# A hand-ordered list of steps that begins at unit 22 instead of unit 19

## The chip, the cores and the metric

The kernel runs on one core of one Trainium2 chip. The metric is the device time of one execution in microseconds.

## The reference

Attention with a position bias for 8 batches and 8 heads of 576 positions with 64 values each, followed by a soft mixture of 8 experts. Everything is float32.

```python
scores = scale * np.matmul(q, k.transpose(0, 1, 3, 2))
x = (psi_rel / psi_i)[..., None]
bias = np.maximum(x @ w1 + b1, 0.0) @ w2
scores = scores + bias.transpose(2, 0, 1)[None, :, :, :]
attn = np.exp(scores - np.max(scores, axis=-1, keepdims=True))
attn = attn / (np.sum(attn, axis=-1, keepdims=True) + 1e-09)
x = np.matmul(attn, v)                       # then laid out as (4608, 512)
logits = x @ phi
d = softmax of logits over the rows          # dispatch
slot_input = d.T @ x                         # 8 experts of 4 slots
slot_out = np.maximum(slot_input[e] @ w1[e], 0.0) @ w2[e]
c = softmax of logits over the slots         # combine
return c @ slot_out
```

## The kernel before

The heads go in four pairs, and a **unit** is one pair of heads of one batch: 32 units, units 0 to 7 for the first pair, 8 to 15, 16 to 23 and 24 to 31 for the last. Ahead of them stand the position biases, which go to DRAM and are read back for each pair; behind them the experts' two layers and the output.

A unit is cut into short named steps, each of one engine (or of SyncE's queue, for transfers):

- `lq`, `lv`: load of q and k (two buffers), of v (two buffers); `wf`: fetch of a block of expert weights, 512 KB, in units 8 to 23; `b0` to `b4`: the bias tiles of the next pair, in its last unit
- for each of five row blocks p: `S` scores (TensorE), `t` bias add and row minimum (VectorE, one for each head), `e` exponential with row sums (ScalarE), `m` reciprocal (VectorE), `n` scaling (GpSimd), `T` and `R` transposes (TensorE), `c`, `cr`, `cR` copies out of PSUM (ScalarE, or VectorE where the mark says so)
- for the two halves: `M0.0` to `M0.4` and `M1.0` to `M1.4`, the products with v (TensorE), `x0`, `x1` copies of the result, and `xs`, the store to the DRAM tensor `xs` for the first three pairs
- for the units of the last pair: `fx`, the read-back of the other pairs' results of that batch, `K`, `L`, `D` and so on for the experts' dispatch
- `w21` to `w36`, filed under unit 31: fetches of weights into buffers of other tiles as these come free

Which block of weights a fetch brings follows from the count of the fetches before it.

All steps are sorted by a place, and the program is issued in that order with no rescheduling, so that each engine's queue is the sorted list of its own steps. The place comes from one of two sources: the list `END`, if the step stands in it (place 1000 and up, in the list's order), or the formula `5 * u + PLAIN[n]`, which lets every unit repeat one pattern, with the end of a unit's work (the M1 steps, whose `PLAIN` is 8.997 to 10.445) among the next unit's first steps.

```python
place, eng = max(rank[u, n] if (u, n) in rank else (5 * u + PLAIN[n][0], PLAIN[n][1]) for n in names.split())
prog.append((place, len(prog), lambda: f(eng)))
...
for _, _, f in sorted(prog, key=lambda x: x[:2]):
    f()
```

In the kernel before, the list names all steps of units 19 to 31, but for the weight fetches of units 22 and 23. Whatever the list does not name stands in front of it. So the last steps of unit 18, `M1.0` to `M1.4`, `x1` and `xs`, all stand in front of the first step of unit 19, and so do the fetches `wf/22` and `wf/23`: the order at that place is

```
... T3/18 cR3/18 c3/18 M1.0/18 M1.1/18 M1.2/18 M1.3/18 M1.4/18 x1/18+ xs/18 wf/22 wf/23
| w21/31 lq/20 lv/19 wf/19 S0/19 S1/19 t0.0/19 t0.1/19 e0.0/19 t1.0/19 S2/19 e0.1/19 fx/24 ...
```

with the list behind the bar. Profile lines: `S` is L379 (L375 for block 4), `t` L392, `e` L399, `m` L407 and L408, `n` L321, `T` and `R` L357, copies L324, `M` L482, `xs` L494, `fx` L505, `lq` L298, `lv` L303, bias tiles L311 to L317, weight fetches L778.

Of the kernel before, what the change touches and what calls it, by code (L numbers as in the profile page):

```python
# [40 lines left out]
}  # L41

END = """
w21/31 lq/20 lv/19 wf/19 S0/19 S1/19 t0.0/19 t0.1/19 e0.0/19 t1.0/19 S2/19 e0.1/19 fx/24 e1.0/19 m0/19 t1.1/19 n0.1/19
e1.1/19 n0.0/19 m1/19 T0/19 t2.0/19 S4/19 n1.0/19 c0/19 t2.1/19 n1.1/19 e2.1/19 R1/19 S3/19 cR1/19+ e2.0/19 t4.0/19
lq/21 t3.0/19 e4.0/19 S0/20 lv/20 t3.1/19 wf/20 T1/19 m4/19 e3.1/19 m2/19 t0.0/20 e3.0/19 n2.1/19 t0.1/20 c1/19
n2.0/19 m3/19 n4.0/19 T2/19 e0.0/20 n4.1/19 S1/20 c2/19 n3.1/19 T4/19 n3.0/19 e0.1/20 t1.0/20 M0.0/19 M0.1/19 c4/19
m0/20 M0.2/19 t1.1/20 e1.0/20 n0.1/20 M0.3/19 M0.4/19 cr4.0/19 n0.0/20 e1.1/20 cr4.1/19+ R3/19 T3/19 x0/19+ cR3/19
S2/20 m1/20 c3/19 n1.0/20 T0/20 n1.1/20 t2.0/20 S4/20 c0/20 t2.1/20 R1/20 e2.1/20 S3/20 cR1/20+ t4.0/20 e2.0/20
M1.0/19 lq/22 t3.0/20 e4.0/20 M1.1/19 t3.1/20 M1.2/19 m4/20 e3.1/20 S0/21 m2/20 e3.0/20 n2.1/20 T1/20 n2.0/20 M1.3/19  # L50
c1/20 t0.0/21 M1.4/19 n4.0/20 t0.1/21 n4.1/20 e0.0/21 T2/20 lv/21 x1/19+ S1/21 wf/21 m3/20 c2/20 xs/19 n3.1/20 T4/20
e0.1/21 n3.0/20 M0.0/20 t1.0/21 M0.1/20 c4/20 m0/21 M0.2/20 e1.0/21 t1.1/21 M0.3/20 n0.1/21 M0.4/20 cr4.0/20 e1.1/21
n0.0/21 cr4.1/20+ R3/20 T3/20 x0/20+ cR3/20 S2/21 m1/21 c3/20 n1.0/21 T0/21 n1.1/21 t2.0/21 S4/21 c0/21 t2.1/21 R1/21
e2.1/21 S3/21 cR1/21+ t4.0/21 e2.0/21 M1.0/20 lq/23 t3.0/21 e4.0/21 M1.1/20 t3.1/21 M1.2/20 m4/21 e3.1/21 S0/22 m2/21
e3.0/21 n2.1/21 T1/21 n2.0/21 M1.3/20 c1/21 t0.0/22 M1.4/20 n4.0/21 t0.1/22 n4.1/21 e0.0/22 T2/21 lv/22 x1/20+ S1/22
m3/21 xs/20 c2/21 n3.1/21 T4/21 e0.1/22 n3.0/21 M0.0/21 t1.0/22 M0.1/21 c4/21 m0/22 M0.2/21 e1.0/22 t1.1/22 M0.3/21
n0.1/22 M0.4/21 cr4.0/21 e1.1/22 n0.0/22 cr4.1/21+ R3/21 T3/21 x0/21+ cR3/21 S2/22 m1/22 c3/21 n1.0/22 T0/22 n1.1/22
t2.0/22 S4/22 c0/22 t2.1/22 R1/22 e2.1/22 S3/22 cR1/22+ t4.0/22 e2.0/22 M1.0/21 t3.0/22 e4.0/22 M1.1/21 t3.1/22
M1.2/21 m4/22 e3.1/22 S0/23 m2/22 e3.0/22 n2.1/22 T1/22 n2.0/22 M1.3/21 c1/22 t0.0/23 M1.4/21 n4.0/22 t0.1/23 n4.1/22
e0.0/23 lq/24 T2/22 lv/23 x1/21+ S1/23 m3/22 c2/22 xs/21 n3.1/22 T4/22 e0.1/23 b2/23 n3.0/22 M0.0/22 t1.0/23 M0.1/22  # L60
c4/22 m0/23 M0.2/22 e1.0/23 t1.1/23 M0.3/22 n0.1/23 M0.4/22 cr4.0/22 e1.1/23 n0.0/23 cr4.1/22+ R3/22 T3/22 x0/22+
cR3/22 S2/23 m1/23 c3/22 n1.0/23 T0/23 n1.1/23 t2.0/23 S4/23 c0/23 t2.1/23 b1/23 R1/23 e2.1/23 S3/23 cR1/23+ t4.0/23
b3/23 e2.0/23 M1.0/22 t3.0/23 e4.0/23 M1.1/22 t3.1/23 M1.2/22 m4/23 e3.1/23 m2/23 lq/25 b0/23 e3.0/23 n2.1/23 T1/23
S2/24 t2.0/24 n2.0/23 M1.3/22 c1/23 M1.4/22 n4.0/23 n4.1/23 t2.1/24 T2/23 S1/24 x1/22+ e2.0/24 T4/23 m3/23 c2/23
e2.1/24 n3.1/23 n3.0/23 M0.0/23 t1.0/24 M0.1/23 c4/23 b4/23 M0.2/23 M0.3/23 t1.1/24 M0.4/23 e1.0/24 cr4.0/23 cr4.1/23+
R3/23 T3/23 x0/23+ e1.1/24 S0/24 cR3/23 m2/24 m1/24 c3/23 t0.0/24 t0.1/24 n2.0/24 n2.1/24 n1.0/24 S3/24 e0.0/24
t3.0/24 M1.0/23 M1.1/23 lv/24 M1.2/23 M1.3/23 M1.4/23 T2/24 e0.1/24 n1.1/24 t3.1/24 m0/24 x1/23+ T1/24 e3.1/24 e3.0/24
m3/24 c2/24 n0.1/24 n0.0/24 T0/24 c0/24 S4/24 R1/24 c1/24+ S0/25 t4.0/24 n3.0/24 n3.1/24 R3/24 cR1/24 cR3/24 T3/24
t0.0/25 c3/24 S2/25 t0.1/25 t2.0/25 e4.0/24 S1/25 M0.0/24 m4/24 M0.1/24 n4.0/24 n4.1/24 M0.2/24 t1.0/25 M0.3/24
t1.1/25 e0.0/25 T4/24 e2.0/25 e0.1/25 e1.1/25 t2.1/25 c4/24+ e2.1/25 cr4.0/24 S3/25 M0.4/24 cr4.1/24 m0/25 e1.0/25  # L70
M1.0/24 t3.0/25 e3.0/25 m1/25 m2/25 t3.1/25 M1.1/24 xs/22 lq/26 lv/25 e3.1/25 x0/24+ M1.2/24 n0.1/25 n0.0/25 n1.1/25
M1.3/24 M1.4/24 n1.0/25 m3/25 x1/24+ T0/25 n2.0/25 R1/25 n2.1/25 c0/25 T1/25 cR1/25+ K01/24 c1/25 S2/26 kc01/24+
t2.0/26 n3.1/25 n3.0/25 t2.1/26 T2/25 S4/25 c2/25 t4.0/25 R3/25 S1/26 cR3/25 e2.1/26 e4.0/25 t1.0/26 S0/26 T3/25
t1.1/26 L/24 m4/25 t0.0/26 M0.0/25 e2.0/26 n4.0/25 M0.1/25 c3/25 n4.1/25 T4/25 t0.1/26 lc/24+ e0.0/26 S3/26 e1.1/26
e0.1/26 m2/26 c4/25+ M0.2/25 cr4.0/25 cr4.1/25+ e1.0/26 D/24 m0/26 t3.0/26 d1/24 m1/26 M0.3/25 M1.0/25 M0.4/25 t3.1/26
n0.1/26 M1.1/25 lv/26 xs/23 M1.2/25 n2.1/26 n2.0/26 n0.0/26 n1.1/26 n1.0/26 e3.0/26 d2/24 M1.3/25 e3.1/26 x0/25+
M1.4/25 dq/24 KR/24 T0/26 K23/24 x1/25+ d3/24 R1/26 krc/24 S4/26 c0/26+ cR1/26 kc23/24 m3/26 t4.0/26 T1/26 lq/27 S2/27
c1/26 T2/26 M0.0/26 M0.1/26 t2.0/27 M0.2/26 lv/27 M0.3/26 W/24 lq/28 c2/26 fx/25 t2.1/27 n3.1/26 M0.4/26 n3.0/26
x0/26+ e4.0/26 m4/26 e2.1/27 T3/26 wc/24 e2.0/27 n4.0/26 R3/26 cR3/26 S0/27 t0.0/27 c3/26 t0.1/27 Z/24 S1/27 zc/24
n4.1/26 e0.0/27 e0.1/27 t1.0/27 K01/25 kc01/25 L/25 t1.1/27 T4/26 lc/25 S3/27 m0/27 c4/26+ K23/25 cr4.0/26+ cr4.1/26+  # L80
t3.0/27 e1.1/27 e1.0/27 D/25 M1.0/26 t3.1/27 kc23/25 M1.1/26 m1/27 m2/27 d1/25 C/24 e3.1/27 e3.0/27 M1.2/26 cA/24
M1.3/26 d2/25 M1.4/26 m3/27 n0.1/27 n0.0/27 n1.0/27 n1.1/27 n2.1/27 n2.0/27 cB/24 dq/25 KR/25 x1/26+ T0/27 n3.1/27
n3.0/27 krc/25+ c0/27 W/25 R1/27 wc/25+ T2/27 S2/28 cR1/27 c2/27 T1/27 fx/26 S4/27 d3/25 t2.0/28 t2.1/28 c1/27 R3/27
cR3/27+ S0/28 t4.0/27 e4.0/27 T3/27 Z/25 t0.0/28 t0.1/28 m4/27 K01/26 c3/27 n4.0/27 S1/28 e0.0/28 zc/25 kc01/26
t1.0/28 L/26 K23/26 e0.1/28 t1.1/28 lc/26 n4.1/27 m0/28 T4/27 kc23/26 c4/27+ cr4.0/27+ cr4.1/27 S3/28 e1.1/28 e1.0/28
e2.0/28 e2.1/28 M0.0/27 D/26 t3.0/28 t3.1/28 C/25 cC/24 m1/28 M0.1/27 n1.1/28 d1/26 M1.0/27 M1.1/27 M0.2/27 e3.1/28
n0.0/28 n0.1/28 M0.3/27 M0.4/27 d2/26 M1.2/27 M1.3/27 n1.0/28 cA/25 M1.4/27 m2/28 e3.0/28 x0/27 d3/26 dq/26+ W/26
# [903 lines left out]
```

## Time and profile before

| | us |
|---|---|
| median of 3 runs | 636.65 |
| lowest and highest | 636.62, 640.1 |
| the profiled execution | 636.0 |
| its span, first to last instruction | 634.2 |

A row gives times in us (mean lengths of one instruction in ns); PE is TensorE, PEld its weight loads, DVE VectorE, ACT ScalarE, POOL GpSimd, SPq SyncE's queue, which issues the DMAs. "Granted clock" is TensorE's clock as a share of full speed. An instruction's row in order of time merges like neighbours (x8: eight of them), and its length then runs from the first to the last.

### The profile page before, as it was taken

What the parts mean: (1) busy time and instruction counts of PE and PEld (TensorE: products, weight loads), DVE (VectorE), ACT (ScalarE), POOL (GpSimd) and SP (SyncE); (2) the same over time, 40 slices, a digit from 0 to 9 for tenths busy, and PEclk for the clock granted to TensorE, in tenths of its full rate; (3) what the DMA queues carried; (4) which work ended last, traced back from release to release, by engine and by line L of the source; (5) the groups of instructions that cost most, each with busy time, mean ns of one, the idle gap of its engine ahead of it and who ended that gap; (6) DMA issues with size and microseconds to landing.
All of it is one profiled execution on the core that took longest, in us unless ns stands there. A gap on an engine that the chain in (4) does not pass through costs nothing.

```text
span 634.2 us, 18241 instructions
## 1 busy us (share of the span) xinstructions
PE 599.0 (94%) x7079; PEld 374.6 (59%) x7079; DVE 427.2 (67%) x1331; ACT 481.8 (76%) x987; POOL 224.7 (35%) x336
## 2 busy tenths in 40 slices
PE   6999699999999999999987999999999999999883
PEld 3444466666666666666654666666666666543452
DVE  7997767767666666666636667677778887664043
ACT  6998788888888888888847888877877778532142
POOL 0000554455555445555424544644314343100000
PEclk9999899999999999999998999999999999999897
DMA  6777222233855453594318326432233137879998
GB/s 237 244 243 251 75 81 82 85 114 117 247 193 169 146 171 128 160 289 133 113 44 337 115 80 179 149 101 64 94 118 118 54 122 244 278 243 352 347 364 299
DMA packets 54694, 110.71 MB, mean 175 GB/s; under 512 B 7120, under 2 KB 24784, under 8 KB 54608
## 3 DMA queue, kind: packets, MB, share of 16 engines
q1 hardware_dynamic: 54608, 109.54, 52.5%
q8 instruction: 56, 0.92, 0.6%
q14 instruction: 30, 0.25, 0.1%
HBM read 82.39 MB, written 27.13 MB: 173 GB/s over the span
## 4 chain that ended last, share of the span: by engine, by line
PE 87%; DVE 4%; ACT 4%; issue 2%; DMA 1%; POOL 1%; SPq 0%; ACTq 0%; POOLq 0%; DVEq 0%
PE ps L482 25%; PE ps L379 20%; PE ps L357 16%; PE ps L274 8%; PE ps L375 6%; PE ps L894 3%; PE ps L869 2%; ACT y L399 2%; PE ps L548 1%; DVE y L392 1%; PE ps L924 1%; PE ps L678 1%; ACT at L324 1%; PE ps L846 1%; DMA tabs<-in_tab_dram 1%
## 5 line engine op out<-in xcount | busy, mean ns | idle before, releaser
L321 POOL TENSOR_SCALAR y<-y,sm 128x576 f32<-128x576 f32 (+1 forms) x320 | 221.9, 707 | 318.6 <-DVE sm L408 194.7
L399 ACT ACTIVATE y<-y,mn 128x576 f32<-128x576 f32 x288 | 222.1, 772 | 37.2 <-DVE sm L407 19.3
L392 DVE CUSTOM_DVE_ANT_0 y<-ps,bm 128x576 f32<-128x576 f32 x256 | 185.2, 754 | 95.5 <-PE ps L357 52.8
L324 ACT COPY at<-ps 128x1024 f32<-128x1024 f32 (+3 forms) x211 | 153.7, 733 | 39.4 <-PE ps L357 31.2
L482 PE MATMUL ps<-at,v 128*64 128x320 f32 (+1 forms) x1280 | 175.3, 413 | 1.3 <-ACT at L324 1.1
L379 PE MATMUL ps<-qk 64*128 64x288 f32 x1024 | 157.3, 423 | 0.0
L357 PEld LDWEIGHTS ps<-ident,y 64*128 64x128 f32 x2624 | 104.4, 139 | 62.5 <-POOL y L321 22.2
L357 PE MATMUL ps<-ident,y 64*128 64x64 f32 x2624 | 119.0, 227 | 10.3 <-POOL y L321 7.8
L482 PEld LDWEIGHTS ps<-at,v 128*64 128x64 f32 x1280 | 83.8, 136 | 61.4 <-issue 9.6
L379 PEld LDWEIGHTS ps<-qk 64*128 64x128 f32 x1024 | 94.4, 189 | 25.6 <-DVE sm L407 9.8
L274 PE MATMUL ps<-f,wbd 128*32 128x512 f32 (+1 forms) x576 | 52.6, 419 | 2.4 <-DVE f L257 2.4
L399 ACT ACTIVATION_READ_ACCUMULATOR y<-y,mn 128x1 f32 x288 | 54.1, 188 | 0.0
L257 DVE TENSOR_SCALAR f<-tabs,scl,nb 128x576 f32<-128x576 f32 x106 | 52.1, 587 | 0.5 <-DMA tabs<-in_tab_dram 0.5
L324 DVE COPY at<-ps 128x256 f32<-128x256 f32 (+3 forms) x77 | 33.7, 442 | 21.7 <-PE ps L357 15.5
L274 PEld LDWEIGHTS ps<-f,wbd 128*32 128x32 f32 x576 | 25.6, 110 | 29.4 <-issue 17.0
L375 PE MATMUL ps<-qk 64*64 64x288 f32 x256 | 39.9, 432 | 0.0
L324 DVE COPY xts<-ps 128x256 f32<-128x256 f32 (+1 forms) x57 | 25.9, 454 | 15.7 <-PE ps L482 12.9
L254 ACT ACTIVATE f<-tabs,cols,scl 128x576 f32<-128x576 f32 x38 | 33.3, 888 | 0.0
L407 DVE TENSOR_SCALAR sm<-sm 128x2 f32<-128x2 f32 (+1 forms) x160 | 28.1, 176 | 3.9 <-ACT y L399 3.3
L408 DVE RECIPROCAL sm<-sm 128x2 f32<-128x2 f32 (+1 forms) x160 | 26.4, 165 | 5.5
L278 ACT ACTIVATE e<-ps,bcon 128x576 f32<-128x576 f32 x36 | 27.2, 757 | 1.6 <-PE ps L274 0.6
L392 DVE CUSTOM_DVE_ANT_0 y<-ps,br 128x576 f32<-128x576 f32 x32 | 24.0, 749 | 1.5 <-PE ps L357 1.0
(147 smaller groups left out, 368.1 us busy)
## 6 DMA issues: line engine op xcount, KB each, us to landing
wt<-in_moe_w_dram SPq DMA_DIRECT2D x64, 512.0 KB, 6.2
qk<-in_qk_dram SPq DMA_DIRECT2D x32, 608.0 KB, 3.8
v<-in_v_dram SPq DMA_DIRECT2D x32, 320.0 KB, 3.3
bias_m<-e SPq DMA_DIRECT2D x32, 288.0 KB, 2.9
out_dram<-ob SPq DMA_DIRECT2D x16, 512.0 KB, 5.2
xs<-xts SPq DMA_DIRECT2D x24, 288.0 KB, 4.8
xo<-xs SPq DMA_DIRECT2D x8, 864.0 KB, 5.7
bm<-bias_m SPq DMA_DIRECT2D x16, 288.0 KB, 4.1
```

The costliest lines, as they stand in the source:

```text
L254: nc.scalar.activation(out=f, in_=tabs[:, s0:s0 + S], func=AF.Relu, bias=cols[:, 1:2], scale=scl[:, sc:sc + 1])
L257: nc.vector.tensor_scalar(out=f, in0=tabs[:, s0:s0 + S], scalar1=scl[:, sc:sc + 1], scalar2=nb1[:, 0:1], op0=ALU.mult, op1=ALU.max)
L274: nc.tensor.matmul(pb[32 * t:32 * t + 32, n, 0:w], wbd, fb[t][:, 512 * n:512 * n + w], start=True, stop=True, tile_position=(0, 32 * t))
L321: nc.gpsimd.tensor_scalar(out=out, in0=y, scalar1=r, scalar2=1.0, op0=ALU.mult, op1=ALU.mult)
L324: (nc.vector.tensor_copy if eng else nc.scalar.copy)(out=out, in_=in_)
L357: nc.tensor.matmul(out, src[rs], ident[rs, rs], is_transpose=True, start=True, stop=True, tile_position=(64 * r, 0))
L375: nc.tensor.matmul(pss[0].t[rs, n, 0:HALF], x[rs, 1152:1216], x[rs, 64 + n * HALF:64 + (n + 1) * HALF], start=True, stop=True, tile_positi ...
L379: nc.tensor.matmul(pss[hh].t[:, n, 0:HALF], x[rs, 640 + p * P:640 + (p + 1) * P], x[rs, k0:k0 + HALF], start=True, stop=True, tile_positio ...
L392: nc.vector.tensor_tensor_reduce(out=d["y", p][:, hs].rearrange("a (x n) -> a x n", x=2), in0=t[:, :, 0:HALF], in1=biases[hp][p][:, hs].re ...
L399: nc.scalar.activation(out=y, in_=y, func=AF.Exp, bias=d["mn", p][:, hh:hh + 1], scale=-1.0, accum_out=d["sm", p][:, hh:hh + 1])
L407: nc.vector.tensor_scalar(out=r, in0=r, scalar1=1e-9, scalar2=None, op0=ALU.add)
L482: nc.tensor.matmul(po[64 * hh:64 * hh + 64], d["v"][:, v0:v0 + 64], main[:, :, 4 * hh + i, :] if i < 4 else rest, start=i == 0, stop=i == ...
```

## The change

Only the text of `END` is changed. The steps of units 19 to 21, the first part of unit 22 and a few of unit 23 are taken out of the list, so that the formula places them; the list now begins at the load of q and k for unit 24, which is issued while unit 23 begins. In front of that load stand `w21/31`, which began the list before, and `fx/24`, the first read-back. `wf/23` is put behind the load of v for unit 23; `wf/22` falls to its place by the formula. All other entries keep their order.

```diff
 END = """
-w21/31 lq/20 lv/19 wf/19 S0/19 S1/19 t0.0/19 t0.1/19 e0.0/19 t1.0/19 S2/19 e0.1/19 fx/24 e1.0/19 m0/19 t1.1/19 n0.1/19
...
-e3.0/22 n2.1/22 T1/22 n2.0/22 M1.3/21 c1/22 t0.0/23 M1.4/21 n4.0/22 t0.1/23 n4.1/22
-e0.0/23 lq/24 T2/22 lv/23 x1/21+ S1/23 m3/22 c2/22 xs/21 n3.1/22 T4/22 e0.1/23 b2/23 n3.0/22 M0.0/22 t1.0/23 M0.1/22
...
+w21/31 fx/24 lq/24 T2/22 lv/23 wf/23 x1/21+ S1/23 m3/22 c2/22 xs/21 n3.1/22 T4/22 e0.1/23 b2/23 n3.0/22 M0.0/22
+t1.0/23 M0.1/22 c4/22 m0/23 M0.2/22 e1.0/23 t1.1/23 M0.3/22 n0.1/23 M0.4/22 cr4.0/22 e1.1/23 n0.0/23 cr4.1/22+ R3/22
...
```

With the formula's places written out, the order around the list's new first entry is

```
... lv/22 wf/22 c1/21 x1/20+ xs/20 S1/22 ... e3.0/22 M1.1/21 M1.2/21 S0/23 m2/22 T1/22 M1.3/21 n2.1/22 n2.0/22
t0.0/23 t0.1/23 n4.0/22 M1.4/21 n4.1/22 c1/22 e0.0/23
| w21/31 fx/24 lq/24 T2/22 lv/23 wf/23 x1/21+ S1/23 m3/22 c2/22 xs/21 n3.1/22 T4/22 e0.1/23 b2/23 ...
```

## Rows read from the trace of the kernel before

**Rows 1.** The page: busy time by engine, and the chain's share by engine

```profile
PE 599.0 (94%) x7079; PEld 374.6 (59%) x7079; DVE 427.2 (67%) x1331; ACT 481.8 (76%) x987; POOL 224.7 (35%) x336
...
PE 87%; DVE 4%; ACT 4%; issue 2%; DMA 1%; POOL 1%; SPq 0%; ACTq 0%; POOLq 0%; DVEq 0%
```

**Rows 2.** SyncE's queue in order of time: start, length (us), line, what is issued

```profile
294.74 0.33 SPq L303 DMA_DIRECT2D v<-in_v_dram  x1
...
308.47 0.33 SPq L303 DMA_DIRECT2D v<-in_v_dram  x1
...
372.05 0.33 SPq L303 DMA_DIRECT2D v<-in_v_dram  x1
...
385.74 0.33 SPq L303 DMA_DIRECT2D v<-in_v_dram  x1
```

**Rows 3.** By stretch: length, each engine's busy time (instructions), TensorE's granted clock, DMA share, GB/s

```profile
102.54:308.47 205.93, 205.93 (x2432) 136.26 (x2434) 138.33 (x481) 180.41 (x376) 104.06 (x151) 1.00 0.50 157
...
294.74:308.47 13.73, 13.73 (x164) 9.09 (x166) 9.20 (x33) 12.02 (x26) 6.93 (x11) 1.00 0.43 130
...
308.47:385.74 77.27, 71.51 (x812) 46.10 (x814) 46.22 (x161) 59.87 (x126) 34.63 (x51) 0.98 0.42 141
...
358.37:372.05 13.68, 13.68 (x164) 9.02 (x166) 9.19 (x33) 12.01 (x26) 6.94 (x11) 1.00 0.44 131
```

**Rows 4.** TensorE in order of time, in brackets the idle time before and its releaser

```profile
327.19 2.91 PE L482 MATMUL ps<-at,v 128*64 128x320 f32 x20 [1.11 <-ACT at L324]
...
335.96 0.82 PE L357 MATMUL ps<-ident,y 64*128 64x64 f32 x16 [1.82 <-POOL y L321]
...
344.48 0.71 PE L357 MATMUL ps<-ident,y 64*128 64x64 f32 x16 [2.15 <-DVE sm L407]
```

**Rows 5.** GpSimd in order of time, the same columns

```profile
334.44 1.47 POOL L321 TENSOR_SCALAR y<-y,sm 128x576 f32<-128x576 f32 x2 [10.57 <-DVE sm L408]
```

**Rows 6.** By stretch, the old join, columns as in rows 3

```profile
331.04:344.73 13.69, 9.72 (x86) 5.94 (x86) 9.65 (x33) 9.03 (x20) 4.71 (x7) 0.88 0.96 353
...
336.00:340.00 4.00, 4.00 (x33) 2.33 (x34) 2.17 (x8) 2.53 (x5) 1.47 (x2) 0.57 1.04 417
```

**Rows 7.** SyncE's queue in order of time, columns as in rows 2

```profile
334.30 0.58 SPq L505 DMA_DIRECT2D xo<-xs  x1
...
372.81 0.33 SPq L494 DMA_DIRECT2D xs<-xts  x1
...
381.11 0.33 SPq L298 DMA_DIRECT2D qk<-in_qk_dram  x1
...
387.86 0.46 SPq L313 DMA_DIRECT2D bm<-bias_m  x1
```

**Rows 8.** DMA issues: line, count, KB each, median us from issue to landing

```profile
wt<-in_moe_w_dram SPq DMA_DIRECT2D x64, 512.0 KB, 6.2
...
qk<-in_qk_dram SPq DMA_DIRECT2D x32, 608.0 KB, 3.8
...
xo<-xs SPq DMA_DIRECT2D x8, 864.0 KB, 5.7
...
bm<-bias_m SPq DMA_DIRECT2D x16, 256.0 KB, 4.5
```

**Rows 9.** TensorE and VectorE in order of time, the first readers behind the new join

```profile
396.98 1.19 PE L379 MATMUL ps<-qk 64*128 64x288 f32 x8
...
398.30 0.76 DVE L392 CUSTOM_DVE_ANT_0 y<-ps,bm 128x576 f32<-128x576 f32 x1 [1.45 <-PE ps L379]
```

**Rows 10.** By stretch, columns as in rows 3

```profile
372.05:385.74 13.69, 13.69 (x164) 9.02 (x166) 9.20 (x33) 12.01 (x26) 6.94 (x11) 1.00 0.30 93
...
385.74:399.44 13.70, 13.70 (x165) 8.87 (x166) 9.23 (x33) 12.03 (x26) 6.94 (x11) 1.00 0.77 227
...
580.00:590.00 10.00, 7.03 (x58) 3.50 (x54) 1.84 (x3) 4.43 (x6) 0.00 (x0) 0.95 1.10 348
...
590.00:600.00 10.00, 9.44 (x140) 4.81 (x134) 0.42 (x1) 0.61 (x2) 0.00 (x0) 0.88 1.11 348
```

More of the change, by code (lines that the diff above doesn't have):

```diff
@@ L43 @@
 END = """
-w21/31 lq/20 lv/19 wf/19 S0/19 S1/19 t0.0/19 t0.1/19 e0.0/19 t1.0/19 S2/19 e0.1/19 fx/24 e1.0/19 m0/19 t1.1/19 n0.1/19
[L45 to L58, printed above, removed]
@@ L59 @@
-M1.2/21 m4/22 e3.1/22 S0/23 m2/22 e3.0/22 n2.1/22 T1/22 n2.0/22 M1.3/21 c1/22 t0.0/23 M1.4/21 n4.0/22 t0.1/23 n4.1/22
-e0.0/23 lq/24 T2/22 lv/23 x1/21+ S1/23 m3/22 c2/22 xs/21 n3.1/22 T4/22 e0.1/23 b2/23 n3.0/22 M0.0/22 t1.0/23 M0.1/22
-c4/22 m0/23 M0.2/22 e1.0/23 t1.1/23 M0.3/22 n0.1/23 M0.4/22 cr4.0/22 e1.1/23 n0.0/23 cr4.1/22+ R3/22 T3/22 x0/22+
-cR3/22 S2/23 m1/23 c3/22 n1.0/23 T0/23 n1.1/23 t2.0/23 S4/23 c0/23 t2.1/23 b1/23 R1/23 e2.1/23 S3/23 cR1/23+ t4.0/23
-b3/23 e2.0/23 M1.0/22 t3.0/23 e4.0/23 M1.1/22 t3.1/23 M1.2/22 m4/23 e3.1/23 m2/23 lq/25 b0/23 e3.0/23 n2.1/23 T1/23
@@ L64 @@
[L64 to L83, printed above, removed]
@@ L84 @@
-cR3/27+ S0/28 t4.0/27 e4.0/27 T3/27 Z/25 t0.0/28 t0.1/28 m4/27 K01/26 c3/27 n4.0/27 S1/28 e0.0/28 zc/25 kc01/26
+w21/31 fx/24 lq/24 T2/22 lv/23 wf/23 x1/21+ S1/23 m3/22 c2/22 xs/21 n3.1/22 T4/22 e0.1/23 b2/23 n3.0/22 M0.0/22
+t1.0/23 M0.1/22 c4/22 m0/23 M0.2/22 e1.0/23 t1.1/23 M0.3/22 n0.1/23 M0.4/22 cr4.0/22 e1.1/23 n0.0/23 cr4.1/22+ R3/22
+T3/22 x0/22+ cR3/22 S2/23 m1/23 c3/22 n1.0/23 T0/23 n1.1/23 t2.0/23 S4/23 c0/23 t2.1/23 b1/23 R1/23 e2.1/23 S3/23
+cR1/23+ t4.0/23 b3/23 e2.0/23 M1.0/22 t3.0/23 e4.0/23 M1.1/22 t3.1/23 M1.2/22 m4/23 e3.1/23 m2/23 lq/25 b0/23 e3.0/23
@@ new lines @@
+n2.1/23 T1/23 S2/24 t2.0/24 n2.0/23 M1.3/22 c1/23 M1.4/22 n4.0/23 n4.1/23 t2.1/24 T2/23 S1/24 x1/22+ e2.0/24 T4/23
+m3/23 c2/23 e2.1/24 n3.1/23 n3.0/23 M0.0/23 t1.0/24 M0.1/23 c4/23 b4/23 M0.2/23 M0.3/23 t1.1/24 M0.4/23 e1.0/24
+cr4.0/23 cr4.1/23+ R3/23 T3/23 x0/23+ e1.1/24 S0/24 cR3/23 m2/24 m1/24 c3/23 t0.0/24 t0.1/24 n2.0/24 n2.1/24 n1.0/24
+S3/24 e0.0/24 t3.0/24 M1.0/23 M1.1/23 lv/24 M1.2/23 M1.3/23 M1.4/23 T2/24 e0.1/24 n1.1/24 t3.1/24 m0/24 x1/23+ T1/24
+e3.1/24 e3.0/24 m3/24 c2/24 n0.1/24 n0.0/24 T0/24 c0/24 S4/24 R1/24 c1/24+ S0/25 t4.0/24 n3.0/24 n3.1/24 R3/24 cR1/24
@@ new lines @@
+cR3/24 T3/24 t0.0/25 c3/24 S2/25 t0.1/25 t2.0/25 e4.0/24 S1/25 M0.0/24 m4/24 M0.1/24 n4.0/24 n4.1/24 M0.2/24 t1.0/25
+M0.3/24 t1.1/25 e0.0/25 T4/24 e2.0/25 e0.1/25 e1.1/25 t2.1/25 c4/24+ e2.1/25 cr4.0/24 S3/25 M0.4/24 cr4.1/24 m0/25
+e1.0/25 M1.0/24 t3.0/25 e3.0/25 m1/25 m2/25 t3.1/25 M1.1/24 xs/22 lq/26 lv/25 e3.1/25 x0/24+ M1.2/24 n0.1/25 n0.0/25
+n1.1/25 M1.3/24 M1.4/24 n1.0/25 m3/25 x1/24+ T0/25 n2.0/25 R1/25 n2.1/25 c0/25 T1/25 cR1/25+ K01/24 c1/25 S2/26
+kc01/24+ t2.0/26 n3.1/25 n3.0/25 t2.1/26 T2/25 S4/25 c2/25 t4.0/25 R3/25 S1/26 cR3/25 e2.1/26 e4.0/25 t1.0/26 S0/26
@@ new lines @@
+T3/25 t1.1/26 L/24 m4/25 t0.0/26 M0.0/25 e2.0/26 n4.0/25 M0.1/25 c3/25 n4.1/25 T4/25 t0.1/26 lc/24+ e0.0/26 S3/26
+e1.1/26 e0.1/26 m2/26 c4/25+ M0.2/25 cr4.0/25 cr4.1/25+ e1.0/26 D/24 m0/26 t3.0/26 d1/24 m1/26 M0.3/25 M1.0/25 M0.4/25
+t3.1/26 n0.1/26 M1.1/25 lv/26 xs/23 M1.2/25 n2.1/26 n2.0/26 n0.0/26 n1.1/26 n1.0/26 e3.0/26 d2/24 M1.3/25 e3.1/26
+x0/25+ M1.4/25 dq/24 KR/24 T0/26 K23/24 x1/25+ d3/24 R1/26 krc/24 S4/26 c0/26+ cR1/26 kc23/24 m3/26 t4.0/26 T1/26
+lq/27 S2/27 c1/26 T2/26 M0.0/26 M0.1/26 t2.0/27 M0.2/26 lv/27 M0.3/26 W/24 lq/28 c2/26 fx/25 t2.1/27 n3.1/26 M0.4/26
@@ new lines @@
+n3.0/26 x0/26+ e4.0/26 m4/26 e2.1/27 T3/26 wc/24 e2.0/27 n4.0/26 R3/26 cR3/26 S0/27 t0.0/27 c3/26 t0.1/27 Z/24 S1/27
+zc/24 n4.1/26 e0.0/27 e0.1/27 t1.0/27 K01/25 kc01/25 L/25 t1.1/27 T4/26 lc/25 S3/27 m0/27 c4/26+ K23/25 cr4.0/26+
+cr4.1/26+ t3.0/27 e1.1/27 e1.0/27 D/25 M1.0/26 t3.1/27 kc23/25 M1.1/26 m1/27 m2/27 d1/25 C/24 e3.1/27 e3.0/27 M1.2/26
+cA/24 M1.3/26 d2/25 M1.4/26 m3/27 n0.1/27 n0.0/27 n1.0/27 n1.1/27 n2.1/27 n2.0/27 cB/24 dq/25 KR/25 x1/26+ T0/27
+n3.1/27 n3.0/27 krc/25+ c0/27 W/25 R1/27 wc/25+ T2/27 S2/28 cR1/27 c2/27 T1/27 fx/26 S4/27 d3/25 t2.0/28 t2.1/28 c1/27
@@ L85 @@
+R3/27 cR3/27+ S0/28 t4.0/27 e4.0/27 T3/27 Z/25 t0.0/28 t0.1/28 m4/27 K01/26 c3/27 n4.0/27 S1/28 e0.0/28 zc/25 kc01/26
 t1.0/28 L/26 K23/26 e0.1/28 t1.1/28 lc/26 n4.1/27 m0/28 T4/27 kc23/26 c4/27+ cr4.0/27+ cr4.1/27 S3/28 e1.1/28 e1.0/28
```

## The prediction

> **What bounds the kernel now.** I read the page first. TensorE is busy for 94% of the span and has 87% of the chain that ended last [rows 1], so anything that stalls another engine counts only where it makes TensorE late. The change touches the order of the steps of units 19 to 22 alone, so the next view is the DMA queue in order of time, which gives a clock for the units. The load of v for unit u waits until the last M1 step of unit u-2 has freed its buffer, so from one such load to the next is one unit. Between 294.74 and 308.47 the loads of units 17 and 18 are 13.73 us apart; between 372.05 and 385.74 those of units 22 and 23 are 13.69 us apart [rows 2]. The first is the formula's order of steps, the second is the listed order.
>
> The view by stretches says the same. Fifteen units in the formula's order, 102.54 to 308.47, take 205.93 us, which is 13.73 each, and TensorE is busy for all 205.93 of them at a granted clock of 1.00. One unit in the listed order takes 13.68 and is filled too. But the five units between the load for unit 18 and the load for unit 23 take 77.27 us, with TensorE busy for 71.51 [rows 3]. Five units at 13.73 are 68.65. So 8.62 us are lost somewhere between unit 18 and unit 22, and nowhere else in this run of units.
>
> TensorE in order of time shows the place. It stands idle 1.11 us at 327.19, 1.82 us at 335.96 and 2.15 us at 344.48, each time for a result of another engine that works on the one unit in flight [rows 4]. That is the join: all steps of unit 18 end, with their five M1 steps at 327 to 330, before the first scores of unit 19 start. In the formula's order the scores, the bias add and the exponentials of the next unit run under the M steps of the last. Here VectorE, ScalarE and GpSimd first run dry (GpSimd waits 10.57 us for its first reciprocals [rows 5]) and then TensorE waits for them.
>
> **What the change does, part by part.** No instruction is added or removed; steps are put in another order, and the two engine marks that the list carries (VectorE or ScalarE for a copy) are the same for units 19 to 22 in list and formula.
>
> *The old join goes.* Units 19 to 22 follow unit 18 as units 1 to 18 follow each other. Price: 8.62 us, less nothing, since I have priced these units at the formula's 13.73 and not at the list's 13.69 (the list's advantage of 0.04 us a unit is in the sum). Of the 8.62, the idle time is 77.27 - 71.51 = 5.76. Another part is the clock: between 336 and 340 the granted clock is 0.57 [rows 6], that is half speed (1.2 instead of 2.4 GHz) for most of it, worth 4.00 x 0.43 = 1.72. The remaining 1.14 are matmuls that count as busy while the pipeline behind them is empty. The Trainium skill, page "TensorE: Matmul & The Clock Gate", section "What's actually happening", has the clock fall after idling and come back with work; by it the 1.72 return with the idle time, and the trace agrees (1.00 in all fifteen filled units, 0.57 right behind the two gaps).
>
> The bounds of this term: if only the idle time came back it would be 5.76; if everything beyond the cadence comes back, 8.62. I take 8.62, since fifteen units in just this order show the cadence with no loss.
>
> *The new join.* The list now takes over in front of the load of q and k for unit 24. I compared the step names on either side of that point. Ahead of it, each engine has the same last steps as it has now at 385.67: TensorE S0, T1, M1.3 and M1.4 and then T2 of unit 22; VectorE t0.0 and t0.1 of unit 23; ScalarE c1 of unit 22 and e0.0 of unit 23; GpSimd n4.0 and n4.1. Behind it the list is the old one, but for two fetches. So the list starts in mid flight, with one unit's softmax under the last unit's M steps, and I put its cost at nothing; the cover is that unit 23's scores are computed before T2 of unit 22 in both orders. If the cover is gone, the old join's price, 8.62, comes back in full.
>
> *The moved transfers.* Four transfers land in another place (the read-back is now issued at 334.30 [rows 7]). The two drifted weight fetches (units 22 and 23) and the fetch into w21's buffer now stand in the old join, and the read-back fx/24 a few steps later. After the change wf/22 stands behind the load of v in unit 22, w21 and fx/24 behind the store xs/20, and wf/23 behind the load of v of unit 23. They are issued by SyncE, whose queue is in order, so what matters is what stands behind them: lq/24 (608 KB, issued at 381.11), the store xs/21, and the bias loads of the next pair, whose first tile is issued in three pieces up to 387.86 [rows 7].
>
> For lq/24: w21 and fx/24 wait for nothing of this unit (a buffer of the pair before last, data stored by units 0, 8 and 16), so SyncE issues them right behind xs/20, at about 373.3 to 374.5 on the old clock, and lq/24 still waits for its own buffer until 381.11. Best case: they have landed by then and cost nothing. Worst case: lq/24 finds both still ahead of it, 512 + 864 KB = 1.41 MB; when the old join's transfers were queued together they moved at 353 GB/s [rows 6], so 4.0 us, and lq/24 lands at 381.11 + 3.8 + 4.0 = 388.9 [rows 7, 8]. Its first reader, S2 of unit 24, starts at 396.98 [rows 9], so 8.1 us are left. I take nothing. For the first bias tile: wf/23 puts 512 KB, 1.5 us, and one issue, 0.5, ahead of it; it lands at 387.86 + 4.5 + 2.0 = 394.4, and its reader t2.0 of unit 24 starts at 398.30 [rows 8, 9]; 3.9 us are left. Also nothing. In sum, unit 22 carries 1.93 MB more in 13.69 us, 141 GB/s on top of 93, that is 234; the unit from 385.74 on moves 227 GB/s now and TensorE is busy for 13.70 of its 13.70 us [rows 10]. So that much traffic does not slow it.
>
> *The order of weights.* The fetches count on, so the blocks numbered 16 to 21 change buffers among themselves. All of them are fetched by unit 23 and read only behind unit 31. Nothing.
>
> *Behind the new join* each engine has the same queue as before, so everything to the end, the tail bound by weight and output transfers included, moves up by the same amount: those transfers wait for buffers that the moved steps free. A loss can hide only in the clock: 580 to 600 show 0.95 and 0.88 [rows 10], 0.5 + 1.2 = 1.7 us, and whether that stretch of half speed falls on waiting or on full work may differ after a shift. I take 0, with 1.7 to either side.
>
> The sum: 636.0 - 8.62 = 627.4 for the profiled execution (span 634.2, so a span of 625.6). The median of the runs is 636.65, which is 0.65 above it, so 628.0 for a median.
>
> **The rivals.**
>
> *The transfers at the new join bite.* Speaks for it: the old join kept the queue at 353 GB/s for 13.69 us [rows 6]. Against it: the two slacks above, 8.1 and 3.9 us after the worst case. It would take the first bias tile being 6 us later instead of 2; the price is then about 2 to 4, 630 to 632.
>
> *The half-speed stretch stays.* If the drop at 336 to 340 is not the idle time's doing, it falls on filled work somewhere and 1.72 of the gain goes: 629.7. The fifteen units at 1.00 speak against it.
>
> *The gap moves.* If the list's first steps leave an engine dry, the change doesn't do what it says: 636 or so. The equal last steps on each engine speak against it.
>
> *The queue is held: slower.* If w21 or fx/24 has to wait on SyncE for something late, lq/24 stands behind it. With 4.0 us of transfers and its own 3.8, lq/24 makes TensorE wait once the queue is let go after 396.98 - 7.8 = 389.2, and each us later is a us lost; the gain is used up at 397.8, and 1% is lost at about 404. What could hold it is fx/24 waiting for the newest store to the same DRAM tensor, xs/20: issued at 372.81 [rows 7], it would be in at about 379. That is 10 us too early to cost anything.
>
> **How the numbers follow.** Old join gone, nothing new: 0.86, with a range of its own of 626.3 to 629.7 (the clock's 1.7 to either side). Transfers 0.05, at 630 to 632. Half speed stays 0.04, at 629.7. The gap moves 0.03, at 636. The queue is held 0.02, at 640. The predicted time is 628.0; the range of 626.3 to 630.9 goes up to the bound at which only the idle time comes back (636.65 - 5.76), takes in the half speed that stays and the cheaper half of the transfers, and leaves out the moved gap, the held queue and some of the first case's edges. About 1% is what a measurement of this kernel can tell from no change, 630.3; faster by more: 0.89, within: 0.09, slower: 0.02.
>
> **What would show it.** Right: the v loads of units 18 to 23 at 13.73 us apart, the last at about 377.1; no idle of TensorE over 0.5 us and a granted clock of 1.00 between 308 and 390; S2 of unit 24 without a wait for qk, and t2.0 of unit 24 without one for bm; a span near 625.6. Wrong: TensorE or VectorE waiting for a DMA behind 377, a new gap at T2 of unit 22 or soon after it, or a tail that is no earlier than now.

## The result and the profile after

The changed kernel took 629.18 us, median of 4 runs (628.42 to 630.81), beside 637.15 for the kernel before: a ratio of 0.9869, 95% interval 0.9832 to 0.9906. Run again later, beside some of the experiments below, it took 628.12 (6 runs, 625.93 to 630.57) against 637.42, a ratio of 0.9855 (0.9825 to 0.9885). The forecast was 628.0. The profiled execution took 628.8 with a span of 627.0; the forecast for its span was 625.6.

Line numbers of the changed kernel are 16 lower than those of the kernel before (S is L363, v's load L287, fx L489); the kernels of the experiments have numbers of their own. SyncE's queue in order of time, the loads of v for units 18 to 23 and the transfers at the new join; columns are start, length, line, what is issued:

```profile
308.22 0.33 SPq L287 DMA_DIRECT2D v<-in_v_dram  x1
...
321.95 0.33 SPq L287 DMA_DIRECT2D v<-in_v_dram  x1
...
363.15 0.33 SPq L287 DMA_DIRECT2D v<-in_v_dram  x1
363.53 0.43 SPq L762 DMA_DIRECT2D wt<-in_moe_w_dram  x1
364.05 0.38 SPq L478 DMA_DIRECT2D xs<-xts  x1
364.49 0.42 SPq L762 DMA_DIRECT2D wt<-in_moe_w_dram  x1
364.96 0.44 SPq L489 DMA_DIRECT2D xo<-xs  x1
372.26 0.33 SPq L282 DMA_DIRECT2D qk<-in_qk_dram  x1
376.89 0.33 SPq L287 DMA_DIRECT2D v<-in_v_dram  x1
```

The loads of v are 13.73 us apart where [rows 2] had 77.27 us for five units: 376.89 - 308.22 is 68.67. The weight fetch of unit 22, the fetch into w21's buffer and the read-back are issued in a row behind unit 22's load of v, and the load of q and k follows 7.3 us later, when its buffer comes free.

By stretch, columns as in [rows 3]:

```profile
308.22:376.89 68.67, 68.67 (x813) 45.47 (x814) 45.99 (x161) 60.12 (x126) 34.69 (x51) 1.00 0.47 151
...
363.15:376.89 13.74, 13.74 (x165) 9.10 (x166) 9.20 (x33) 12.03 (x26) 6.95 (x11) 1.00 0.69 234
376.89:390.63 13.74, 13.74 (x164) 8.93 (x166) 9.22 (x33) 12.03 (x26) 6.95 (x11) 1.00 0.84 270
```

The first row answers to the third of [rows 3]: TensorE was busy for 71.51 of 77.27 us at a mean granted clock of 0.98, and is now for 68.67 of 68.67 at 1.00. The other two are the units on either side of the new join; they carry 234 and 270 GB/s and TensorE has no idle time in either.

Where the 7.2 us between the two spans went, by marks that both traces have (the load of v for units 18, 23 and 31, the first product of the experts' first layer and of their second, the end):

| stretch | before | after | difference |
|---|---|---|---|
| start to load of v, unit 18 | 308.47 | 308.22 | -0.25 |
| unit 18 to unit 23 | 77.27 | 68.67 | -8.60 |
| unit 23 to unit 31 | 140.19 | 140.26 | +0.07 |
| unit 31 to first layer | 36.82 | 36.86 | +0.04 |
| first layer to second layer | 26.72 | 27.17 | +0.45 |
| second layer to the end | 44.73 | 45.84 | +1.11 |

The marks of the last four rows, of the kernel before and then of the changed one:

```profile
525.93 0.43 SPq L303 DMA_DIRECT2D v<-in_v_dram  x1
...
562.75 0.64 PE L869 MATMUL ps<-wt,sT 128*32 128x512 f32 x4 [0.41 <-ACT sT L131]
...
589.47 1.08 PE L894 MATMUL ps<-wt,hT 128*32 128x256 f32 x8 [0.68 <-ACT hT L131]
```

```profile
517.15 0.42 SPq L287 DMA_DIRECT2D v<-in_v_dram  x1
...
554.01 0.64 PE L853 MATMUL ps<-wt,sT 128*32 128x512 f32 x4 [0.41 <-ACT sT L115]
...
581.18 1.08 PE L878 MATMUL ps<-wt,hT 128*32 128x256 f32 x8 [0.68 <-ACT hT L115]
```

So the units gave what was forecast, 8.60, and the tail took 1.6 back. Two stretches around the second layer's start, first of the kernel before and then of the changed one, show what differs there. They do not begin at the same distance from that start, but each holds the whole of the fall in the clock there:

```profile
588.00:598.00 10.00, 9.19 (x132) 4.68 (x132) 0.00 (x0) 0.67 (x2) 0.00 (x0) 0.83 1.10 347
```

```profile
578.00:588.00 10.00, 8.56 (x92) 4.51 (x96) 0.00 (x0) 1.17 (x2) 0.00 (x0) 0.66 1.10 348
```

A granted clock of 0.83 over ten us is 3.4 us at half speed (1.2 instead of 2.4 GHz), 0.66 is 6.8 us. The two kernels run the same instructions in the two layers, beside transfers at 347 and 348 GB/s; the 3.4 us more at half speed are worth up to 1.7 us, and the tail is 1.6 us longer. Other profiles bear this out: in the one of the transfers late (below) the granted clock is 1.00 from 580 to 610, and the first layer takes 26.72 us there as in the kernel before; in the second profile of the changed kernel, with 6.8 us at half speed again, it takes 27.17 as in the first.

```profile
555.94:582.66 26.72, 23.75 (x185) 9.44 (x185) 10.81 (x23) 6.68 (x10) 0.00 (x0) 1.00 1.08 344
```

```profile
553.40:580.57 27.17, 24.20 (x185) 9.73 (x185) 10.82 (x23) 6.69 (x10) 0.00 (x0) 0.96 1.06 343
```

### The profile page after: what moved, and what is told of

It reads as the page before. It is cut to its first block, busy times and chain, and to the rows that moved or that the text cites. A ratio compares the mean times of both kernels' runs of the same rounds, so it can differ in the third digit from the quotient of the medians.

```text
span 627.0 us, 18249 instructions
## 1 busy us (share of the span) xinstructions
PE 597.5 (95%) x7079; PEld 374.5 (60%) x7079; DVE 427.1 (68%) x1331; ACT 482.1 (77%) x987; POOL 224.8 (36%) x336
## 3 DMA queue, kind: packets, MB, share of 16 engines
HBM read 82.39 MB, written 27.13 MB: 175 GB/s over the span
## 4 chain that ended last, share of the span: by engine, by line
PE 89%; DVE 3%; ACT 3%; issue 1%; DMA 1%; SPq 0%; ACTq 0%; DVEq 0%
PE ps L466 25%; PE ps L363 21%; PE ps L341 16%; PE ps L258 8%; PE ps L359 6%; PE ps L878 3%; PE ps L853 2%; ACT y L383 1%; PE ps L532 1%; PE ps L908 1%; PE ps L662 1%; PE ps L830 1%; DVE y L376 1%; DMA tabs<-in_tab_dram 1%; ACT at L308 0%
## 5 line engine op out<-in xcount | busy, mean ns | idle before, releaser
L363 PE MATMUL ps<-qk 64*128 64x288 f32 x1024 | 157.4, 423 | 0.0
L363 PEld LDWEIGHTS ps<-qk 64*128 64x128 f32 x1024 | 93.9, 189 | 25.2 <-DVE sm L391 10.8
L258 PE MATMUL ps<-f,wbd 128*32 128x64 f32 (+1 forms) x576 | 52.6, 420 | 2.5 <-DVE f L241 2.5
L359 PE MATMUL ps<-qk 64*64 64x288 f32 x256 | 38.4, 418 | 0.0
```

The lines of the kernel that those rows point to most:

```text
L258: nc.tensor.matmul(pb[32 * t:32 * t + 32, n, 0:w], wbd, fb[t][:, 512 * n:512 * n + w], start=True, stop=True, tile_position=(0, 32 * t))
L359: nc.tensor.matmul(pss[0].t[rs, n, 0:HALF], x[rs, 1152:1216], x[rs, 64 + n * HALF:64 + (n + 1) * HALF], start=True, stop=True, tile_positi ...
L363: nc.tensor.matmul(pss[hh].t[:, n, 0:HALF], x[rs, 640 + p * P:640 + (p + 1) * P], x[rs, k0:k0 + HALF], start=True, stop=True, tile_positio ...
```

## The experiments

Three accounts of the gain stood against each other at the start. The join theory: unit 18 was drained before unit 19 began, and that alone cost 8.6 us. The transfer theory: the old join held three weight fetches, the read-back and two loads in one place, and taking 2.5 MB out of it was the gain. A third, the order theory, gives it to the formula's order within a unit.

### The transfers alone (e1_transfers_only)

The edit is shown against the kernel before:

```diff
-w21/31 lq/20 lv/19 wf/19 S0/19 S1/19 t0.0/19 ... S2/19 e0.1/19 fx/24 e1.0/19
+lq/20 lv/19 wf/19 S0/19 S1/19 t0.0/19 ... S2/19 e0.1/19 e1.0/19
...
+lv/22 wf/22
...
-lq/24 T2/22 lv/23
+w21/31 fx/24 lq/24 T2/22 lv/23 wf/23
```

> The kernel before with its join at unit 19 kept, and only the four moved transfers (two drifted weight fetches, the fetch into w21's buffer, the first read-back) put where the change has them. Join theory: TensorE runs dry at the join as before, the five units up to the load of v for unit 23 still take about 77.3 us, the time stays within 1.5 us of before (ratio 0.998 to 1.002). Transfer theory (the gain came from taking 2.5 MB out of the join): about 629, ratio near 0.987.

Measured: 637.99 us (10 runs) against 637.8 (20 runs), a ratio of 1.0015 (0.9984 to 1.0046). By stretch, and TensorE in order of time:

```profile
310.72:388.00 77.28, 71.54 (x812) 45.87 (x814) 46.22 (x161) 59.86 (x126) 34.46 (x51) 0.98 0.42 135
```

```profile
329.42 2.91 PE L481 MATMUL ps<-at,v 128*64 128x320 f32 x20 [1.10 <-ACT at L323]
...
338.19 0.71 PE L356 MATMUL ps<-ident,y 64*128 64x64 f32 x16 [1.81 <-POOL y L320]
...
346.76 0.71 PE L356 MATMUL ps<-ident,y 64*128 64x64 f32 x16 [2.15 <-DVE sm L406]
```

The five units take 77.28 us with the transfers gone, against 77.27 with them, and the three gaps are those of [rows 4] to a hundredth. The transfers had no measurable part in the loss.

### The join alone (e2_join_only)

The edits from here on are against the changed kernel, unless another is named:

```diff
+EARLY = {(22, "wf"): 94.996, (23, "wf"): 94.997, (31, "w21"): 94.998, (24, "fx"): 96.683}
...
+        place = EARLY.get((u, names), place)
         prog.append((place, len(prog), lambda: f(eng)))
```

> The changed kernel with the four transfers put back to where the kernel before has them (at the start of unit 19), the order of all other steps as changed. Join theory: the five units take 68.7 us, the time is that of the changed kernel, about 629 (ratio 0.985 to 0.990): 2.9 MB at the start of unit 19 are hidden under a filled unit. Transfer theory: TensorE waits at unit 19 or 20 and most of the 8 us are lost again, 635 to 637.

Measured: 628.28 us (4 runs), a ratio of 0.9887 (0.9845 to 0.9929; the quotient of the two medians, 628.28 and 637.8, is 0.985). By stretch, the five units and the first of them:

```profile
308.88:377.49 68.61, 68.61 (x813) 45.32 (x814) 45.99 (x161) 60.09 (x126) 34.55 (x51) 1.00 0.49 159
308.88:322.61 13.73, 13.73 (x165) 9.06 (x166) 9.21 (x33) 12.03 (x26) 6.91 (x11) 1.00 0.70 245
```

With the transfers back at their old place and the join gone, the five units take 68.61 us and TensorE is filled, with 245 GB/s beside it in the first of them. The whole gain belongs to the join.

### The list's order without a join (e3_list_no_join)

Against the kernel before, in excerpts:

```diff
-w21/31 lq/20 lv/19 wf/19 S0/19 S1/19 t0.0/19 t0.1/19 e0.0/19 ...
+M1.0/17 lq/20 t3.0/18 e4.0/18 M1.1/17 t3.1/18 M1.2/17 m4/18 e3.1/18 S0/19 m2/18 e3.0/18 n2.1/18 T1/18 n2.0/18
+M1.3/17 c1/18 t0.0/19 M1.4/17 n4.0/18 t0.1/19 n4.1/18 e0.0/19 T2/18 lv/19 wf/19 x1/17+ S1/19 ...
```

The list's own pattern of units 20 and 21 was carried back, so that it begins in the middle of unit 18.

> Units 19 to 22 stay in the order of the list, but the list is carried back to the middle of unit 18 by its own pattern, so that no unit is drained; the transfers as in the change. Join theory: what was lost was the drained unit and not the list's order within a unit; 13.69 us a unit for some four to five units, so 0.2 us below the changed kernel, about 629 (ratio 0.985 to 0.989). Theory that the formula's order itself is the gain: 635 to 637.

Measured: 631.0 us (5 runs, 629.14 to 631.7), a ratio of 0.9913 (0.9881 to 0.9946; the quotient of the medians is 0.989). By stretch, the five units:

```profile
308.71:377.18 68.47, 68.47 (x812) 45.11 (x814) 45.99 (x161) 60.06 (x126) 34.52 (x51) 1.00 0.48 152
```

Within the units the expectation held: 68.47, 0.2 below the changed kernel. So what cost 8.6 us was never the list's order but the place where it began, and the order theory falls. The time as a whole did not come as expected: 2 to 3 us above the changed kernel's where 0.2 below was expected. The two intervals overlap, and the trace puts nothing of it into units 18 to 23: the profiled span is 627.4 against 627.0, and beyond the load of v for unit 31 TensorE waits 0.5 us for the last read-back and 1.1 us for the combine weights, waits that the changed kernel's trace does not have. Such waits do not belong to this order alone: the trace of the join alone has 1.4 us for the last read-back, and that of the join put back (below) 1.1 for each of the two, in the formula's order. Nor can this trace show the whole excess, for it is of the fastest of the five runs, at a mean granted clock of 0.988; the other four had 0.983 and 0.984. Whether the rest comes with this order was not settled.

### The join put back (e4_join_back)

```diff
+    def late(u, n):
+        return 6 * sum(u - 2 * (n == "lq") >= first for first in (19,))
...
-        place, eng = max(rank[u, n] if (u, n) in rank else (5 * u + PLAIN[n][0], PLAIN[n][1]) for n in names.split())
+        place, eng = max(rank[u, n] if (u, n) in rank else (5 * u + late(u, n) + PLAIN[n][0], PLAIN[n][1]) for n in names.split())
```

> The changed kernel, with the formula's places of unit 19 and later moved up by 6, so that unit 18 ends before unit 19 starts; order within units, list and transfers' neighbours as in the change. Join theory: 8.6 us come back, 5.8 of them idle time of TensorE between units 18 and 20, and the granted clock falls to half for some 3 to 4 us behind it: 636 to 638 (ratio 0.998 to 1.003). Transfer or order theory: stays at 629.

Measured: 638.9 us (10 runs) against 637.8, a ratio of 1.0029 (1.0005 to 1.0052). By stretch, the five units and the place of the drop; then TensorE in order of time:

```profile
309.68:387.02 77.34, 71.59 (x813) 46.07 (x814) 46.23 (x161) 59.88 (x126) 34.45 (x51) 0.98 0.41 134
338.00:343.00 5.00, 5.00 (x33) 2.88 (x30) 2.83 (x10) 3.34 (x7) 1.05 (x2) 0.66 0.10 12
```

```profile
328.37 2.91 PE L469 MATMUL ps<-at,v 128*64 128x320 f32 x20 [1.10 <-ACT at L308]
...
337.13 0.71 PE L344 MATMUL ps<-ident,y 64*128 64x64 f32 x16 [1.81 <-POOL y L305]
...
345.68 0.71 PE L344 MATMUL ps<-ident,y 64*128 64x64 f32 x16 [2.14 <-DVE sm L394]
```

One number added to the formula's places brings the whole loss back: 77.34 us, the same three gaps, and 1.7 us of lost clock (5.00 x 0.34) behind the second of them. The DMA moves 12 GB/s in that stretch, where the old join's moved 417 [rows 6].

### Two joins (e5_two_joins)

The same edit with `(11, 19)`.

> The changed kernel with two drained joins, at units 11 and 19, where the run before had one at 19. Join theory: the price is one of the join, not of the place: each takes about 5.8 us of idle TensorE plus what the drained pipeline and a half-speed stretch add, so two are 14 to 17 us above the changed kernel, 643 to 647 (ratio 1.008 to 1.015). Theory that the loss belongs to the transfers around unit 19, or to the last store before it: the join at 11 costs little and the time is that of one join, 637 to 639.

Measured: 646.82 us (4 runs), a ratio of 1.0147 (1.0115 to 1.0179). By stretch, from the load of v for unit 10 to that for unit 17, with the join at 11; the five units with the join at 19; and the clock behind each:

```profile
199.16:303.89 104.73, 99.05 (x1136) 64.58 (x1138) 64.68 (x225) 83.95 (x176) 48.27 (x71) 0.98 0.49 161
...
317.61:394.95 77.34, 71.59 (x812) 46.18 (x814) 46.22 (x161) 59.86 (x126) 34.44 (x51) 0.98 0.40 134
226.00:231.00 5.00, 4.37 (x36) 2.74 (x37) 2.52 (x8) 3.02 (x7) 2.04 (x3) 0.66 0.23 94
346.00:351.00 5.00, 5.00 (x36) 2.97 (x34) 2.86 (x8) 3.28 (x7) 0.98 (x2) 0.66 0.09 14
```

The same seven units of the join put back, which has none at 11:

```profile
199.94:295.96 96.02, 96.02 (x1136) 63.39 (x1138) 64.42 (x225) 84.16 (x176) 48.30 (x71) 1.00 0.56 175
```

The join at 11 costs 104.73 - 96.02 = 8.71 and the one at 19 77.34 - 68.67 = 8.67. The price goes with draining a unit, at both places tried. Together 17.4, a little above the 14 to 17 that were expected; the medians differ by 18.7 (646.82 - 628.12), the rest within what runs of one kernel differ by.

### The transfers late (e6_transfers_late)

```diff
-w21/31 fx/24 lq/24 T2/22 lv/23 wf/23 x1/21+ S1/23
+lq/24 T2/22 lv/23 w21/31 fx/24 wf/22 wf/23 x1/21+ S1/23
```

> The changed kernel with all four moved transfers, 1.5 MB of weights and the read-back of 0.9 MB, put behind the load of v for unit 23, in front of the first bias tile of the next pair. In the changed kernel that tile lands at 385.06 and its reader starts at 389.49, 4.4 us later. The three transfers added in front take 1.93 MB / 353 GB/s = 5.5 us and 1.5 us of issue. Theory that transfers cost only what goes beyond their slack: the bias add waits 1 to 2.6 us for the tile, and TensorE behind it up to as much: 629 to 632. Theory that transfers beside a filled unit slow TensorE in themselves: more than 3 us, 632 and above. Theory that they are free: no wait, 629.

Measured: 627.98 us (4 runs), a ratio of 0.9851 (0.9819 to 0.9883). The first bias tile's first piece, issued at 380.5, landed after 10.2 us, at 390.7. VectorE and TensorE in order of time, and two units of this kernel by stretch:

```profile
390.85 0.76 DVE L375 CUSTOM_DVE_ANT_0 y<-ps,bm 128x576 f32<-128x576 f32 x1 [2.11 <-POOL y L304]
...
391.60 0.76 DVE L375 CUSTOM_DVE_ANT_0 y<-ps,bm 128x576 f32<-128x576 f32 x1
```

```profile
391.76 0.72 PE L340 MATMUL ps<-ident,y 64*128 64x64 f32 x16 [0.47 <-DVE mn L375]
```

```profile
377.59:405.42 27.83, 27.36 (x336) 18.46 (x338) 17.92 (x62) 23.14 (x49) 14.41 (x21) 1.00 0.77 253
```

and the same two units of the changed kernel:

```profile
376.89:404.02 27.13, 27.13 (x336) 18.07 (x338) 17.84 (x62) 23.14 (x49) 14.49 (x21) 1.00 0.59 188
```

VectorE's wait is put down to GpSimd, whose queue holds the same work as in the changed kernel; what is new in front of the add is the late bias tile. The tile comes in three pieces, the first for one head and the other two for the other. The add of the first head starts 0.16 us after its piece landed, and that of the second again 0.16 us after the last piece (issued at 381.54, in after 9.9 us, at 391.44). So the tile was what they waited for; this is read from the times, not tested by a run of its own. In the changed kernel it starts 12.60 us behind the load of v (389.49 - 376.89), here 13.26, so 0.7 us late; TensorE stands idle 0.47 us, and the two units are 0.70 us longer (27.83 - 27.13). The piece came 5.7 us later against the load of v (390.69 - 377.59 = 13.10, against 384.26 - 376.89 = 7.37), near the 5.5 us that 1.93 MB take at 353 GB/s, and it had had 5.2 us to spare. So 1.93 MB more in front of the tile used up its slack and cost only what went beyond it. Of the 1 to 2.6 us expected the trace shows less, since the expectation had counted the slack from the tile's last piece, 4.4 us, and at its upper end had added 1.5 us of issue; and the median shows none of it: a loss of 0.7 is below what runs of one kernel differ by.

### The last read-back first (e7_last_read_first)

```diff
-w28/31 cr4.1/31 K23/30 T3/31 kc23/30+ fx/31
+cr4.1/31 K23/30 T3/31 kc23/30+ fx/31 w28/31
```

> The changed kernel with one weight fetch (w28) put behind the last read-back, fx/31, in place of just in front of it. In the profiles so far the last read-back lands 26.2 to 27.8 us after the last load of v and TensorE waits 0.5 to 1.4 us for it whenever that is later than about 26.5. Theory that part of what was short of the forecast is this race: the read-back lands about 1.5 us earlier, no wait for it, 0.3 to 0.8 us in the mean. Theory that the rest is the clock alone: no difference.

> The changed kernel once more, beside the others: 629, ratio 0.985 to 0.990; its spread between runs goes with the granted clock (627 at 0.989, 631 at 0.981), as the twenty runs of the kernel before do (633.8 at 0.991, 642.8 at 0.976).

Measured: 628.21 us (6 runs), a ratio of 0.985 (0.9823 to 0.9878), beside 628.12 and 0.9855 for the changed kernel run again. The landing of the last read-back in this kernel, and in the changed kernel, took

```profile
DMA to landing us min/median/max: 7.4/7.4/7.4
```

```profile
DMA to landing us min/median/max: 7.2/7.2/7.2
```

both from an issue at 536.3. So moving the fetch neither let the read-back be issued earlier nor made it land sooner, and the expectation of 1.5 us earlier fell. No difference was measured. The six runs of the changed kernel went from 625.93 us at a mean granted clock of 0.992 to 630.57 at 0.981, so time and clock went together as expected.

## Why the prediction was right

**The cadence.** The forecast rested on a unit that is filled by its neighbours taking 13.73 us in the formula's order and 13.69 in the list's. The five units after (68.67) and those of the experiment with the list's order and no join (68.47) show both numbers again. The term of 8.62 came out as 8.60. The choice between 5.76, the idle time alone, and 8.62, everything beyond the cadence, was the right one. The half-speed part came out as said: all five drained joins that were profiled (before, transfers alone, join back, and the two of two joins) have a granted clock of 0.57 to 0.66 over the four or five us right behind the second gap, 1.7 us each, and none of the filled stretches of units 18 to 23 has it: removing the gaps removed it. The two idle stretches in front of the fall were 1.1 and 1.8 us long. The Trainium skill's page "TensorE: Matmul & The Clock Gate" ("What's actually happening") has the clock fall after idling; these runs agree. The last 1.14 us of the 8.62, which the forecast put down to an empty pipeline, came back too, but no run shows what they were.

**The new join.** It was put at nothing, because every engine has the same last steps there in both orders. That was right: TensorE is busy for 13.74 of 13.74 us on either side of it.

**The moved transfers.** The load of q and k for unit 24 was nearly at the better of the two bounds: issued at 372.26 it landed in 3.8 us, the median of [rows 8], though the read-back, issued at 364.96, was in after 8.4 us, at 373.4, and so still on its way for 1.1 us. The first bias tile was forecast 2.0 us later behind the fetch of unit 23 with 3.9 us left; its first piece, which its first reader needs, landed at 384.26, its last at 385.06, and that reader

```profile
389.49 0.76 DVE L376 CUSTOM_DVE_ANT_0 y<-ps,bm 128x576 f32<-128x576 f32 x1 [1.45 <-PE ps L363]
```

started 5.2 us after the first and 4.4 us after the last, waiting for TensorE as before [rows 9]. The experiment with the transfers late shows that this slack was real: 1.93 MB more used it up and cost 0.7 us.

**The rivals.** The gap did not move and the queue was not held: fx/24 was issued 0.5 us behind w21 without waiting for the store before it. The rival that the half speed stays was wrong for the join, but a cousin of it accounts for the difference between a span of 627.0 and the forecast 625.6: the tail had 6.8 us at half speed where it had 3.4 before. The forecast had named that stretch and given it 1.7 us to either side; the table above shows 1.6 given back in it, in the rows of the two layers. Whether this comes with the change stays open. Both profiles of the changed kernel have 6.8 us there, and so have those of the join alone and of the last read-back first. The profiles of the kernel before and of the three kernels with a join at 19 have 3.4, but so has that of the list's order without a join, and that of the transfers late has none.

**Luck in the number.** The term that was worked out, 8.62, was met to 0.02. That the second median of the changed kernel, 628.12, lies 0.1 from the forecast is in part chance: the forecast started from a median of three runs, 636.65, and more runs of the kernel before gave 637.42 and 637.8; the gain against these is 9.3 to 9.7, and in the first measurement it was 8.0.

## What to carry to other kernels

Where an order is stitched from two sources, cut it at a moment and not at a unit: a list that starts with the first step of a unit, behind the last step of the unit before, is a barrier, and here it cost 8.6 to 8.7 us each time, two thirds of it idle time of the bounding engine, a fifth clock, the rest unexplained. Look for it as one period in the regular issue times of a load that is longer than its neighbours, and price it by the cadence and not by the idle time. Transfers that are moved with it cost what goes beyond the slack of the first reader behind them. Both the slack and the queue's rate can be read from the trace before; take the slack from the piece of the transfer that this reader needs.

## What the runs showed of the hardware that was not expected

The spread between runs of one program goes mostly with the clock. Twenty runs of the kernel before went from 633.78 us, at a mean granted clock of 0.991, to 642.75 at 0.976; time and clock correlate at -0.92. The time multiplied by the clock is what would be left if all of the time at half speed had fallen on work. Its median over those twenty runs is 626.6, and over the changed kernel's second six 620.1, 6.5 us apart; the time at half speed has a median of 21.7 and 16.3 us, which by the same reckoning costs 10.8 and 8.2, 2.7 apart. So some 6.5 of the gain are work and waiting and up to 2.7 are clock, beside 6.9 (8.62 - 1.72) and 1.72 in the forecast. The clock's part is an upper bound, since some of the half speed falls on time in which TensorE waits.
